# One batch's theta and weight transposes in another order, two casts on another engine, and the last tile cut three to one

## The chip, the cores and the metric

The kernel runs on one core of a Trainium2 chip. The metric is the device time of one execution in microseconds (us). Four timed runs of the kernel before gave 169.96, 170.08, 170.22 and 171.64 us, a median of 170.15. A core has a matrix engine (PE, whose weight loads are listed apart as PEld), a vector engine (DVE), a scalar engine (ACT), GpSimd (POOL) and SyncE (SP), which in this kernel only issues DMAs. Each engine works through its own queue in order.

## What is computed

The inputs are q, k and v (4 batches, 8 heads, 768 tokens, 64 per head) and four weight matrices, all float32. First comes a retention (a linear attention with a decay for each head), whose output for all heads of a token is its row of x, 512 wide:

```
for t in range(S):
    state = gamma * state + outer(k[t], v[t])      # per batch and head, 64 x 64
    y[t]  = scale * q[t] @ state
x = y, heads side by side                          # (4, 768, 512)
```

Then a mixing layer:

```
theta  = x @ w_theta
zr, zi = x * cos(theta), x * sin(theta)
u      = x + w_tok_r @ zr + w_tok_i @ zi           # over the tokens of a batch
out    = u + relu(u @ w_ch)
```

## The kernel before, in words

**Tiling.** A batch's 768 tokens are 6 chunks of 128, or 3 pairs of chunks. There are 12 pairs in all, n = 0 to 11; pair n belongs to batch n // 3. The output is made in 24 tiles of 128 tokens, m = 0 to 23. Matrix work is in bf16 with float32 sums in PSUM. The program writes out the order by hand: each engine runs its instructions in the order in which the calls below stand, and the semaphore waits are put in by the framework.

**A pair.** `load` (L76) brings k, q and v of a pair, 512 KB each, all through SP's queue, into a ring of seven buffers (`pair`). `prep` (L162) makes bf16 copies: k is only cast, by one engine (ACT L169, or POOL or DVE L171); q and v are multiplied by a decay factor in two halves (L175), and the pair of engines given says who takes each half: DP is DVE and POOL, PP is POOL twice. `flip` (L179) transposes k or q on PE and copies the result on DVE; from pair 7 on k, and from pair 10 on q, is transposed by a DMA instead (`flip_dma`, L193). `ret_A` and `ret_mask` make the masked scores, `ret_Y` multiplies them with v, `ret_I` adds the part from the state, `ret_S` and `state_out` update the state. `ret_out` (L278) copies the two halves of the transposed x out of PSUM. `x_pe` (L294) turns x into rows on PE, or `x_dma` (L288) with a DMA for pairs from 5 on. `theta` (L309) is four matmuls and two sines on ACT; `zmul` (L319), on DVE, makes the z of one chunk.

**A tile.** `moe_M(m, lo, hi)` (L327) is the token mix: for each of a batch's six chunks two matmuls 512 columns wide (L340). It needs the transposed token weights of its tile (`w_flip`, L390, and `w_out`, L399: DVE for the real part, ACT for the imaginary one, unless told otherwise) and z of the chunk. `moe_u` (L344, DVE L347) adds x. u is transposed on PE (`moe_U`) or by a DMA (`moe_U_dma`, L350), `moe_O` (L365) multiplies by w_ch, `moe_out` (L372, DVE) finishes, `store` (L378, SP) writes. The PSUM tile of `moe_M` has one buffer for most tiles, so a tile's first matmul waits until `moe_u` of the tile before it has read that buffer. Transposes and `moe_O` share two PSUM buffers, tag `tr`.

**The order.** L469 to L569 are the start: pairs 0, 1, 2 (batch 0), with pieces of tile 0 and 1 between them, and the preparation of pair 3. From L579 a loop over n = 3 to 12 does pair n beside the finishing of pair n-1 and one or two tiles of an earlier batch: one tile each at n = 3 to 6 (tiles 2 to 5, with tiles 0 and 1 finished at n = 3), two each from n = 7 (tiles 6 and 7 at n = 7, tile 8 and 9 at n = 8, and so on). In each round SP's queue gets, in this order: the DMA transpose of the next k (from n = 6), the load of k of pair n+3, `x_dma(n-1)` (from n = 6), the load of q, the load of v, a store. At the end of a round DVE gets `zmul(n-1, 0)` and `zmul(n-1, 1)`, then, in rounds with two tiles, `moe_u` of the second tile. After the loop the last tiles follow, and `moe_last` (L407) does tile 23, cut in two column halves so that the last steps overlap.

**Lines the prediction touches.** In the start: L547 to L557 (second `ret_Y` of pair 2, its `ret_out`, `w_tok(1)`, chunks 2 and 3 of tile 0, `theta(2, 0)`, `flip(3, "k")`, `theta(2, 1)`). In the loop: L598 to L601 (k, q and v of pair n+1 at the head of the round), L657 to L660 (the same at n = 3), L670 and L671 (k of pair n+2 on ACT). In the tail: L407 to L457.

Of the kernel before, what the change touches and what calls it, by code (L numbers as in the profile page):

```python
# [14 lines left out]
FT = mybir.dt.float32  # L15
BF = mybir.dt.bfloat16
# [16 lines left out]
def kernel(  # L33
# [17 lines left out]
    nc = tc.nc  # L51
    B, H, S, D = q.shape
    dm = H * D
    P = 128
    HP = P // 2
    nT = S // P
    nD = dm // P
# [3 lines left out]
    nG = nT // 2  # L61
# [158 lines left out]
    def ret_Y(n, two):  # L220

        if two == 0:
            st[n, "y"] = [psum.tile([P, NP, P], FT, name="yT_ps", tag="acc", bufs=2)
                          for _ in range(2)]
        yT, at, vp = st[n, "y"], st[n, two], st[n, "v"]
        for j in range(NP):
            for a in range(2):
                half = slice(a * HP, (a + 1) * HP)
                for par in range(2):
                    h = 2 * j + par  # L230
                    nc.tensor.matmul(yT[a][par * D:(par + 1) * D, j, :],  # L231
                                     vp[half, two, h * D:(h + 1) * D],
                                     at[half, par, j, :],
                                     start=(two == 0 and j == 0),
                                     stop=(two == 1 and j == NP - 1),
                                     skip_group_check=True)

    def ret_I(n, a):

        c = 2 * (n % nG) + a  # L240
        half = slice(a * HP, (a + 1) * HP)
        yT = st[n, "y"][a]
        if c > 0:
            for j in range(NP):
                nc.tensor.matmul(yT[:, j, :], stbd[c % 2][:, j, :],  # L245
                                 st[n, "qT"][:, :, j, half], start=False,
                                 stop=False, skip_group_check=True)
# [71 lines left out]
    def zmul(n, a):  # L319
        b, g = divmod(n, nG)  # L320
        c = 2 * g + a
        nc.vector.tensor_mul(zs[b][:, c], st[n, "cs", a], _bcast_mid(xs[b][:, c, :], 2))  # L322
# [80 lines left out]
    def w_tok(t0):  # L403
        for r in range(2):
            w_flip(r, t0)

    def moe_last(m):  # L407

        b, t0 = divmod(m, nT)
        hw = dm // 2  # L410
        y_ps = [psum.tile([P, hw], FT, name="y_ps", tag="y", bufs=1),
                psum.tile([P, hw], FT, name="y_ps", tag="acc", bufs=2)]
        u = work.tile([P, dm], BF, name="u", bufs=5)
        uT = work.tile([P, nD, P], BF, name="uT", bufs=4)

        def prods(e):
            for s0 in range(nT):
                for r in range(2):
                    nc.tensor.matmul(y_ps[e], wT[r][:, s0, t0 * P:(t0 + 1) * P],  # L419
                                     zs[b][:, s0, r, e * hw:(e + 1) * hw],  # L420
                                     start=(s0 == 0 and r == 0),
                                     stop=(s0 == nT - 1 and r == 1))
            nc.vector.tensor_add(u[:, e * hw:(e + 1) * hw], y_ps[e],
                                 xs[b][:, t0, e * hw:(e + 1) * hw])

        def flip_u(e):
            u_ps = psum.tile([P, 2, P], BF, name="u_ps", tag="tr", bufs=2)
            for j in range(2):
                jj = 2 * e + j
                nc.tensor.transpose(u_ps[:, j, :], u[:, jj * P:(jj + 1) * P], ident)  # L430
            nc.scalar.copy(uT[:, 2 * e:2 * e + 2, :], u_ps)  # L431

        moe_U_dma(m - 1)
        prods(0)
        moe_O(m - 2)
        moe_out(m - 2)
        store(m - 2)
        prods(1)
        flip_u(0)
        moe_O(m - 1)  # L440
        moe_out(m - 1)
        store(m - 1)
        flip_u(1)
        o_ps = [psum.tile([P, hw], FT, name="o_ps", tag="st", bufs=1),
                psum.tile([P, hw], FT, name="o_ps", tag="acc", bufs=2)]
        for js in ((0, 1), (2, 3)):
            for e in range(2):
                for j in js:
                    nc.tensor.matmul(o_ps[e], uT[:, j, :],
                                     wch[:, j, e * hw:(e + 1) * hw], start=(j == 0),  # L450
                                     stop=(j == nD - 1))
        for e in range(2):
            ot = work.tile([P, hw], FT, name="oh", bufs=2)
            nc.vector.scalar_tensor_tensor(ot, o_ps[e], 0.0, u[:, e * hw:(e + 1) * hw],
                                           ALU.max, ALU.add)
            (nc.sync, nc.scalar)[e].dma_start(
                out=out[b, t0 * P:(t0 + 1) * P, e * hw:(e + 1) * hw], in_=ot)  # L457
# [86 lines left out]
    ret_Y(2, 0)  # L544
    ret_I(2, 0)
    ret_I(2, 1)
    ret_Y(2, 1)  # L547
    ret_out(2, 0, AC.copy)
    ret_out(2, 1, DV.tensor_copy)
    zmul(1, 1)  # L550
    w_tok(1)
    moe_M(0, 2, 3)
    prep(3, "k", (PL,))
    moe_M(0, 3, 4)
    theta(2, 0)
    flip(3, "k")
    prep(3, "q", DP)  # L557
    theta(2, 1)
    x_pe(2)
    w_flip(0, 2, False)  # L560
    w_out(0, 2, AC.copy)
# [17 lines left out]
    for n in range(nG, B * nG + 1):  # L579
        mine, done = tiles_of[n], tiles_of[n - 1]  # L580
        late, two = n > nG, len(mine) > 1
        nxt = n + 1 in pairs

        if nxt and n + 1 >= K_DMA:
            flip_dma(n + 1, "k")
        if n + 3 in pairs:
            load(n + 3, "k")
        if n >= U_DMA:
            moe_U_dma(done[1])
        def preps(engines):  # L590
            prep(n + 1, "q", engines)
            prep(n + 1, "v", PP)
            if n in (nG, nG + 1):
                w_cast(n - nG + 4)

        if n == nG:
            nc.gpsimd.tensor_copy(wch, wdma["ch"])
        if n == nG + 1:  # L598
            prep(n + 1, "k", (PL,))
        if nxt and n > nG:  # L600
            preps(PP)  # L601
        if late:
            ret_I(n - 1, 1)

        if n in pairs:
            ret_A(n, 0)
            ret_mask(n, 0)
        if n == nG:
            moe_M(0, 5, nT)
            w_flip(1, 2)  # L610
            moe_u(0)
            moe_M(1, 4, nT)
            moe_u(1)
        if late:
            ret_Y(n - 1, 1)
            ret_S(n - 1, 1)
            ret_out(n - 1, 0, nc.scalar.copy)
            ret_out(n - 1, 1, nc.scalar.copy)
            state_out(n - 1, 1)
            if n - 1 >= X_DMA:  # L620
                x_dma(n - 1)
        if n + 3 in pairs:
            load(n + 3, "q")

        first = mine[0]
        moe_M(first, 0, 3 if two else 2)
        if late:
            theta(n - 1, 0)
            if n - 1 < X_DMA:
                x_pe(n - 1)  # L630
            theta(n - 1, 1)
        if two:
            moe_M(first, 3, nT)
            moe_u(first)
        for name, limit in (("k", K_DMA), ("q", Q_DMA)):
            if nxt and nG + 1 < n + 1 < limit:
                flip(n + 1, name)
        if n + 1 >= K_DMA and not two:
            moe_M(first, 2, 4)
        if nxt and n + 1 >= Q_DMA:  # L640
            flip_dma(n + 1, "q")
        if n + 3 in pairs:
            load(n + 3, "v")
        for t in tiles_of[n - 2]:
            store(t)
        if n + 1 >= U_DMA:
            moe_U_dma(first)

        if n in pairs:
            ret_S(n, 0)  # L650
            state_out(n, 0)
            ret_A(n, 1)
            ret_mask(n, 1)
            ret_Y(n, 0)
            ret_I(n, 0)
        if n < U_DMA:
            moe_U(done)  # L657
        if n == nG:
            prep(n + 1, "k", (AC,))
            preps(DP)  # L660
        if n == nG or n + 1 < K_DMA and not two:
            moe_M(first, 2, 4)
        if n < nG + 3:
            w_tok(n - nG + 3)
        if not two:
            moe_M(first, 4, nT)
            moe_u(first)
        elif n in pairs:
            moe_M(mine[1], 0, nT)
        if n + 2 in pairs and n > nG:  # L670
            prep(n + 2, "k", (AC,))  # L671
        if late:
            zmul(n - 1, 0)
            zmul(n - 1, 1)
        if two and n in pairs:
            moe_u(mine[1])
        for i, t in enumerate(done):
            if n == nG:
                flip(n + 1, "kq"[i])
            moe_O(t)  # L680
            moe_out(t)
        if n not in pairs:
            moe_M(mine[1], 0, nT)
            moe_u(mine[1])
# [43 lines left out]
```

## Time and profile before

One execution was profiled. Its own time is 170.84 us, of which the trace's span is 169.1; the other 1.74 us lie around the span.

| | |
|---|---|
| median of four timed runs | 170.15 us |
| profiled execution | 170.84 us, span 169.1 |
| PE busy | 155.9 us, 92% of the span |
| DVE, ACT, POOL busy | 101.5, 80.1, 65.7 us |
| read and written in HBM | 25.69 and 6.29 MB |
| k cast on POOL (L171) | 3 times, 1.04 us each |
| k cast on ACT (L169) | 9 times, 1.05 us each |
| half of q on DVE, on POOL (L175) | 5 times 0.91 us, 19 times 1.12 us |
| DMA transpose of x (`x_dma`) | 7, median 3.3 us from issue to landing |

How to read it: "busy" counts the instructions of an engine, not the time in which it waits. A wait in a row of the timeline stands in brackets behind it, with what ended it. The chain of waits goes back from the last instruction of all to what released it, step by step; what isn't in the chain did not set the end. PE is busy nearly throughout, so what counts is where it isn't, and who ended each of those gaps.

### The profile page before, as it was taken

How to read it: one execution, taken by the hardware profiler on the slowest of the kernel's cores; microseconds unless marked ns; L12 is line 12 of the kernel's file. 1: busy time of each engine (PE TensorE's matmuls, PEld its weight loads, DVE VectorE, ACT ScalarE, POOL GpSimd, SP SyncE). 2: the span in 40 equal slices, each digit the busy share in tenths (PEclk: the TensorE clock that was granted, in tenths of full speed). 3: DMA queues.
4: the chain of work that ended last, by engine and by line, in shares of the span. 5: the costliest groups of instructions: out<-in, count | busy, mean ns of one | idle time of the engine just before them, and what ended most of it. 6: DMA issues, size and time to landing. Idle time of an engine off the chain costs nothing.

```text
span 169.1 us, 4659 instructions
## 1 busy us (share of the span) xinstructions
PE 155.9 (92%) x1949; PEld 88.9 (53%) x1975; DVE 101.5 (60%) x137; ACT 80.1 (47%) x138; POOL 65.7 (39%) x83
## 2 busy tenths in 40 slices
PE   7969897698999999999997999999999999999990
PEld 2345665464666667555653654555545544444560
DVE  2358897969584687854926672864727435344451
ACT  8216567371719776696835727547083350000010
POOL 6274859685696787480727144000000000000000
PEclk9999999999999999999999999999999999999997
DMA  4999999989999999999999998959645161753433
GB/s 126 306 342 311 322 330 351 291 305 305 310 305 325 288 264 309 312 197 296 230 293 223 281 277 175 232 65 241 61 94 139 31 186 31 232 113 93 134 116 126
DMA packets 66789, 37.92 MB, mean 224 GB/s; under 512 B 24144, under 2 KB 61264, under 8 KB 66768
## 3 DMA queue, kind: packets, MB, share of 16 engines
q1 hardware_dynamic: 66624, 37.50, 87.3%
q8 instruction: 15, 0.25, 0.6%
q10 hardware_dynamic: 144, 0.13, 0.2%
q14 instruction: 6, 0.05, 0.1%
HBM read 25.69 MB, written 6.29 MB: 189 GB/s over the span
## 4 chain that ended last, share of the span: by engine, by line
PE 77%; DVE 10%; DMA 6%; issue 2%; POOL 1%; DVEq 0%; SPq 0%; POOLq 0%
PE y_ps L340 33%; PE o_ps L368 11%; PE th_ps L312 11%; PE at_ps L208 4%; PE kq_ps L183 3%; DMA pair<-in_q_dram 3%; DVE z L322 3%; PE yT_ps L231 3%; DMA x_sb<-xT 3%; DVE at L215 3%; PE st_ps L262 3%; PE yT_ps L245 3%; PE w_ps L393 2%; DVE kqT L187 2%; PE y_ps L419 2%
## 5 line engine op out<-in xcount | busy, mean ns | idle before, releaser
L340 PE MATMUL y_ps<-z,wtr 128*128 128x512 bf16 x133 | 50.5, 379 | 3.0 <-DVE u L347 1.1
L340 PE MATMUL y_ps<-z,wti 128*128 128x512 bf16 x122 | 46.2, 379 | 0.4 <-issue 0.2
L175 POOL TENSOR_TENSOR kqb<-pair,qscp 128x512 bf16<-128x512 f32 x19 | 21.0, 1121 | 29.3 <-DMA pair<-in_q_dram 22.0
L215 DVE TENSOR_TENSOR at<-at_ps,maskp 128x1024 bf16<-128x1024 f32 x24 | 29.2, 1219 | 4.4 <-PE at_ps L208 4.4
L347 DVE TENSOR_TENSOR u<-y_ps,x_sb 128x512 bf16<-128x512 f32 x23 | 15.9, 690 | 25.0 <-PE y_ps L340 24.9
L175 POOL TENSOR_TENSOR kqb<-pair,vscp 128x512 bf16<-128x512 f32 x24 | 25.5, 1084 | 3.5 <-DMA pair<-in_v_dram 3.5
L285 ACT CAST xT<-yT_ps 128x512 bf16<-128x512 f32 x20 | 13.4, 736 | 28.3 <-PE yT_ps L231 28.3
L312 PE MATMUL th_ps<-wth,xT 128*128 128x512 bf16 x93 | 23.2, 379 | 0.2
L375 DVE SCALAR_TENSOR_TENSOR ot<-o_ps,u 128x512 f32<-128x512 f32 x23 | 15.8, 689 | 12.4 <-PE o_ps L368 12.3
L368 PE MATMUL o_ps<-wch,uT 128*128 128x512 bf16 x92 | 22.8, 379 | 0.2
L340 PEld LDWEIGHTS <-wti 128*128 128x128 bf16 x138 | 13.5, 98 | 15.5 <-issue 2.4
L322 DVE TENSOR_TENSOR z<-cs,x_sb 128x1024 bf16<-128x1024 bf16 x24 | 17.8, 771 | 5.8 <-DMA x_sb<-xT 5.7
L276 ACT CAST stbd<-st_ps 64x256 bf16<-64x256 f32 x40 | 14.7, 367 | 13.3 <-PE st_ps L262 12.4
L315 ACT ACTIVATE cs<-th_ps,halfpi 128x512 bf16<-128x512 f32 x24 | 16.5, 688 | 9.4 <-PE th_ps L312 8.9
L340 PEld LDWEIGHTS <-wtr 128*128 128x128 bf16 x138 | 13.5, 98 | 13.6
L316 ACT ACTIVATE cs<-th_ps,zerob 128x512 bf16<-128x512 f32 x24 | 16.5, 686 | 0.0
L312 PEld LDWEIGHTS <-xT 128*128 128x128 bf16 x96 | 9.0, 98 | 10.6 <-DVE xT L285 0.6
L368 PEld LDWEIGHTS <-uT 128*128 128x128 bf16 x92 | 8.8, 98 | 10.3 <-ACT uT L361 0.4
L187 DVE COPY kqT<-kq_ps 128x1024 bf16<-128x1024 bf16 x16 | 10.8, 686 | 4.8 <-PE kq_ps L183 4.8
L208 PE MATMUL at_ps<-kqT 64*64 64x128 bf16 x384 | 10.6, 221 | 2.6 <-DVE at L215 1.8
L431 ACT COPY uT<-u_ps 128x256 bf16<-128x256 bf16 x2 | 0.7, 372 | 25.5 <-PE u_ps L430 25.5
L183 PEld LDWEIGHTS <-kqb 128*128 128x128 bf16 x136 | 8.7, 99 | 5.3 <-DVE kqb L175 0.8
(61 smaller groups left out, 166.7 us busy)
## 6 DMA issues: line engine op xcount, KB each, us to landing
pair<-in_k_dram SPq DMA_DIRECT2D x12, 512.0 KB, 7.0
pair<-in_q_dram SPq DMA_DIRECT2D x12, 512.0 KB, 7.6
pair<-in_v_dram SPq DMA_DIRECT2D x12, 512.0 KB, 7.8
out_dram<-ot SPq DMA_DIRECT2D x23, 256.0 KB, 2.4
wtok<-in_moe_w_tok_r_dram SPq DMA_DIRECT2D x6, 384.0 KB, 6.6
wtok<-in_moe_w_tok_i_dram SPq DMA_DIRECT2D x6, 384.0 KB, 6.4
w<-in_moe_w_theta_dram SPq DMA_DIRECT2D x1, 1024.0 KB, 8.1
w<-in_moe_w_ch_dram SPq DMA_DIRECT2D x1, 1024.0 KB, 8.6
```

The source lines that it names most:

```text
L175: engines[two].tensor_mul(dst[:, two], src[:, two], _bcast_last(sc[:, 2 * g + two], D))
L208: nc.tensor.matmul(at_ps[half, par, j, :], kT[rows, two, j, half], qT[rows, :, j, half], start=(j == 0), stop=(j == NP - 1), skip_group_ch ...
L215: nc.vector.tensor_mul(at.rearrange("p a j t -> p (a j) t"), at_ps.rearrange("p a j t -> p (a j) t"), _bcast_mid(maskp[:, two].rearrange(" ...
L276: nc.scalar.copy(stbd[(c + 1) % 2][sl, :, sl], st_ps[b][sl])
L312: nc.tensor.matmul(th_ps, st[n, "xT"][:, a, j, :], wth[:, j, :], start=(j == 0), stop=(j == NP - 1))
L315: nc.scalar.activation(cs[:, 0, :], th_ps, AF.Sin, bias=halfpi, scale=1.0)
L316: nc.scalar.activation(cs[:, 1, :], th_ps, AF.Sin, bias=zerob, scale=1.0)
L322: nc.vector.tensor_mul(zs[b][:, c], st[n, "cs", a], _bcast_mid(xs[b][:, c, :], 2))
L340: nc.tensor.matmul(y_ps, wT[r][:, s0, t0 * P:(t0 + 1) * P], zs[b][:, s0, r, :], start=(s0 == 0 and r == 0), stop=(s0 == nT - 1 and r == 1))
L347: nc.vector.tensor_add(u, mo[m]["y"], xs[b][:, t0, :])
L368: nc.tensor.matmul(o_ps, mo[m]["uT"][:, j, :], wch[:, j, :], start=(j == 0), stop=(j == nD - 1))
L375: nc.vector.scalar_tensor_tensor(ot, mo[m]["o"], 0.0, mo[m]["u"], ALU.max, ALU.add)
```

## The change

Three edits.

1. *Start.* The PE transposes of the token weights for tile 1 stand before the second `ret_Y` of pair 2, and their copies out of PSUM behind the two `ret_out`. The matmuls of tile 0 with chunk 3 go behind `theta(2, 1)`. The cast of k of pair 3 stands a few lines earlier, at the same place of POOL's own queue.
2. *Loop, n = 4 and 5.* q and v of pairs 5 and 6 (and k of 5) are no longer prepared at the head of the round but behind `ret_out` and `state_out`; half of q goes to DVE (two instructions that POOL did). The cast of k of pair 6 goes from ACT, at the end of round 4, to POOL, in round 5. On DVE the new half of q stands behind the first mask of the round and ahead of the copy of `x_pe`. On POOL the order is k, half of q, v, weight casts. No DMA is moved on SP's queue; the loads of v of pairs 7 and 8 wait for DVE too, as their buffers held the q that DVE now reads.
3. *Last tile.* Cut in 384 and 128 columns of y and u in place of 256 and 256; u's transposes are three and one, and the last matmuls take three and one. The output's halves stay 256 wide.

```diff
     def moe_last(m):
-        hw = dm // 2
-        y_ps = [psum.tile([P, hw], FT, name="y_ps", tag="y", bufs=1),
-                psum.tile([P, hw], FT, name="y_ps", tag="acc", bufs=2)]
+        cut = (nD - 1) * P
+        cols = (slice(0, cut), slice(cut, dm))
+        y_ps = [psum.tile([P, cut], FT, name="y_ps", tag="y", bufs=1),
+                psum.tile([P, P], FT, name="y_ps", tag="acc", bufs=2)]
...
-                                     zs[b][:, s0, r, e * hw:(e + 1) * hw],
+                                     zs[b][:, s0, r, cols[e]],
...
-            nc.vector.tensor_add(u[:, e * hw:(e + 1) * hw], y_ps[e],
-                                 xs[b][:, t0, e * hw:(e + 1) * hw])
+            nc.vector.tensor_add(u[:, cols[e]], y_ps[e], xs[b][:, t0, cols[e]])
-        def flip_u(e):
-            u_ps = psum.tile([P, 2, P], BF, name="u_ps", tag="tr", bufs=2)
-            for j in range(2):
-                jj = 2 * e + j
-                nc.tensor.transpose(u_ps[:, j, :], u[:, jj * P:(jj + 1) * P], ident)
-            nc.scalar.copy(uT[:, 2 * e:2 * e + 2, :], u_ps)
+        def flip_u(lo, hi):
+            u_ps = psum.tile([P, hi - lo, P], BF, name="u_ps", tag="tr", bufs=2)
+            for j in range(lo, hi):
+                nc.tensor.transpose(u_ps[:, j - lo, :], u[:, j * P:(j + 1) * P], ident)
+            nc.scalar.copy(uT[:, lo:hi, :], u_ps)
...
-        flip_u(0)
+        flip_u(0, nD - 1)
...
-        flip_u(1)
+        flip_u(nD - 1, nD)
...
-        for js in ((0, 1), (2, 3)):
+        for js in (range(nD - 1), (nD - 1,)):
...
     ret_I(2, 1)
+    w_flip(0, 1, False)
+    w_flip(1, 1, False)
     ret_Y(2, 1)
     ret_out(2, 0, AC.copy)
     ret_out(2, 1, DV.tensor_copy)
+    w_out(0, 1)
+    w_out(1, 1)
     zmul(1, 1)
-    w_tok(1)
+    prep(3, "k", (PL,))
     moe_M(0, 2, 3)
-    prep(3, "k", (PL,))
-    moe_M(0, 3, 4)
     theta(2, 0)
     flip(3, "k")
     prep(3, "q", DP)
     theta(2, 1)
+    moe_M(0, 3, 4)
     x_pe(2)
...
-        if n == nG + 1:
-            prep(n + 1, "k", (PL,))
-        if nxt and n > nG:
+        if nxt and n > nG + 2:
             preps(PP)
...
             state_out(n - 1, 1)
+            if n < nG + 3:
+                prep(n + 1, "k", (PL,))
+                preps(DP)
...
-        if n + 2 in pairs and n > nG:
+        if n + 2 in pairs and n > nG + 1:
             prep(n + 2, "k", (AC,))
```

More of the change, by code (lines that the diff above doesn't have):

```diff
@@ L442, in moe_last @@
         store(m - 1)
-        flip_u(1)
+        flip_u(nD - 1, nD)
+        hw = dm // 2
         o_ps = [psum.tile([P, hw], FT, name="o_ps", tag="st", bufs=1),
                 psum.tile([P, hw], FT, name="o_ps", tag="acc", bufs=2)]
-        for js in ((0, 1), (2, 3)):
+        for js in (range(nD - 1), (nD - 1,)):
             for e in range(2):
```

## The prediction, made before the changed kernel was run

> **What bounds the kernel now.** I read the page first, then the chain of waits in order of time, then SP's own timeline, then the timelines of PE, DVE and POOL around the places that are edited.
>
> ```profile
> PE 155.9 (92%) x1949; PEld 88.9 (53%) x1975; DVE 101.5 (60%) x137; ACT 80.1 (47%) x138; POOL 65.7 (39%) x83
> PE   7969897698999999999997999999999999999990
> DMA  4999999989999999999999998959645161753433
> ```
>
> PE is the bound, but the DMA engines are full for the first 60% of the span (each digit is a slice of 4.2 us). The digits can't say which of the two sets the end; the chain does:
>
> ```profile
> 82.35 0.41 PE kq_ps L183 x8
> 82.76 4.97 DMA x_sb<-xT
> 88.08 0.34 issue
> 88.43 0.68 DVE z L322
> 89.11 0.61 DVE u L347
> 89.77 0.38 PE y_ps L340
> ```
>
> From 43 us to the end the chain is PE throughout except here, in round n = 8. PE's first matmul of tile 8 waits 1.10 us (88.67 to 89.77) for `moe_u` of tile 7, which stands on DVE behind two `zmul` of pair 6, and these wait for the DMA transpose of pair 6's x, landed at 87.7. Whether PE could be there earlier doesn't matter, unless that DMA is earlier. SP's timeline (start, duration) says why it is not:
>
> ```profile
> 76.25 0.38 SPq L81 DMA_DIRECT2D pair<-in_q_dram  x1
> 76.69 0.89 SPq L81 DMA_DIRECT2D pair<-in_v_dram  x1
> 77.69 1.36 SPq L380 DMA_DIRECT2D out_dram<-ot  x1
> 79.15 2.88 SPq L195 DMA_TRANSPOSE kqT<-kqb  x1
> 82.12 0.53 SPq L81 DMA_DIRECT2D pair<-in_k_dram  x1
> 82.76 2.02 SPq L290 DMA_TRANSPOSE x_sb<-xT  x1
> ```
>
> SP's rows stand end to end, here and back to 0.8 us. Pair 6's xT was ready when ACT ended its copies (77.71 + 1.32 = 79.03), its transpose was issued 3.7 us later: the queue was late, not the data. So up to 89.77 a lead of PE is worth nothing and a loss of up to 1.10 us costs nothing.
>
> One more landing binds, in round 3: q of pair 4, for which POOL waited 1.46 us and DVE started at the same moment.
>
> ```profile
> 44.43 1.59 POOL L175 TENSOR_TENSOR kqb<-pair,qscp 128x512 bf16<-128x512 f32 x1 [1.46 <-DMA pair<-in_q_dram]
> 44.43 0.68 DVE L175 TENSOR_TENSOR kqb<-pair,qscp 128x512 bf16<-128x512 f32 x1
> ```
>
> **The change, part by part.**
>
> *Start.* PE is idle twice here: 0.55 us before `ret_Y(2, 1)`, and 0.78 before chunk 3 of tile 0:
>
> ```profile
> 30.92 0.42 PE L231 MATMUL yT_ps<-at,kqb 64*64 64x128 bf16 x16 [0.55 <-DVE at L215]
> 33.10 0.38 PE L340 MATMUL y_ps<-z,wtr 128*128 128x512 bf16 x1 [0.78 <-DVE z L322]
> ```
>
> The 12 transposes take 0.67 us (the chain's row at 56.97, "PE w_ps L393 x12") and fill the first gap: 30.37 to 31.04, so `ret_Y` starts 0.12 later and ends at 31.44. The two copies to xT (0.75, on ACT and DVE at once) end at 32.25. Meanwhile PE does chunk 2 (two matmuls of 0.216, z ready at 31.46) to 31.9, and waits to about 32.3 for xT. Then theta 0.86 (33.15), `flip(3, "k")` 0.45 (33.6; POOL's cast ended at 32.51, ACT's copy that frees the PSUM buffer ends at 33.0), theta 0.86 (34.45), chunk 3 0.43 (34.9). Its z is ready in time: DVE does xT to 32.25, the weight copy 0.54, z 0.68 to 1.00, that is 33.8 at the latest. The next step, `x_pe(2)`, stood at 35.70: a lead of 0.8. Behind the DVE work that follows it may grow to 1.2 by the end of tile 1, as chunk 5 of tile 0 (39.88, released by a z of 1.22 us) moves with DVE.
>
> In round 3 the lead meets q of pair 4. DVE can't start its half before 44.43 and ends it at 45.11; behind it in DVE's queue is the copy of tile 3's weights (45.24 before, now 45.11, to 45.67), which frees the PSUM buffer that `flip(4, "k")` needs: 45.75 in place of 46.31. So 0.55 of the lead is left. Both ends: nothing, if DVE's order gives no more than the 0.13; 1.2, if q lands sooner. I take 0.55, the sum of the rows.
>
> *Rounds 4 and 5.* POOL loses two halves of q (1.12 each) and gains one cast of k (1.04); ACT loses a cast (1.05) at 58.37; DVE gains two halves (0.68 to 0.91). SP's order is the same. Pair 5's q landed when POOL started on it (51.70), and POOL's two halves ended at 53.74, just before the transposes of q (54.07). With a lead of 0.55 PE would have waited about 0.3; halves side by side end by 52.8. So this part keeps the lead, and brings nothing of itself: PE has no gap above 0.16 between 50 and 70. What DVE's half is put ahead of: the copy of `x_pe(4)`. First mask to 50.9 with the lead, q 51.7 to 52.4, the copy can start at 52.4, where `x_pe` ends: no delay. In round 5 the copy (62.73 before) can be late by 0.3, as the new cast of k on POOL (58.05 to 59.09) falls beside the two z (59.15 before): z beside a busy POOL took up to 1.68 in place of 1.28 for two (68.92). PE would wait those 0.3 before `flip(6, "q")`. Cost at the end: nothing, since round 8 covers 1.10 + 0.55 = 1.65 us; without that cover, 0.3. The two loads that now wait for DVE's halves were issued at 60.31 and 66.16, 8 and 3 us after the halves end. ACT's free 1.05 is worth nothing: its next copies (60.20) waited for PE.
>
> The Trainium skill ("SBUF — State Buffer", the section on engine ports) says that DVE with two SBUF inputs and GpSimd take a shared port by an exclusive lock, the second waiting out the first. The z of 1.22 and 1.53 us (against 0.68) beside POOL's casts agree. By that rule each z of round 4 could lose the whole 1.04 of the cast; it would still lie under round 8.
>
> *Round 8.* x of pair 6 lands at 87.7, DVE's two z and u follow (89.71), PE starts tile 8 at 89.77 as before. The gap of 1.10 becomes 1.65. The start's and the rounds' parts are worth 0 at the end.
>
> *Last tile.* Here all counts:
>
> ```profile
> 162.94 1.03 PE L368 MATMUL o_ps<-wch,uT 128*128 128x512 bf16 x4
> 163.92 1.24 PE L449 MATMUL o_ps<-wch,uT 128*128 128x256 bf16 x8
> 164.01 0.69 DVE L375 SCALAR_TENSOR_TENSOR ot<-o_ps,u 128x512 f32<-128x512 f32 x1 [0.55 <-PE o_ps L368]
> 164.98 0.76 DVE L454 SCALAR_TENSOR_TENSOR oh<-o_ps,u 128x256 f32<-128x256 f32 x2 [0.28 <-PE o_ps L449]
> ```
>
> Matmuls 256 wide follow at 0.109, 512 wide at 0.216, transposes (128 wide, each with its own weights) at 0.056. So 12 x 384 columns take 1.95 and 12 x 128 take 0.67: 2.62, as 2 x 1.31 before. `moe_O(21)` moves from 160.66 to 161.30, its `moe_out` on DVE from 161.72 to 162.36 and ends at 163.05. `moe_O(22)` takes the PSUM buffer that this frees: 163.10 in place of 162.94, ending its issue at 163.97. One transpose 0.06; ACT's last copy (128x128, 0.27 by the line through 0.372 for 256 and 0.585 for 512) ends at 164.50. Six last matmuls of 0.109 run from 164.02 to 164.67, so the 0.19 that PE waited for ACT (164.36 to 164.55) is gone, and the last two end their issue at 164.89, 0.1 earlier than before. On DVE `moe_out(22)` moves from 164.01 to 164.16, ends at 164.85, and the first output half starts at 165.00 in place of 164.98. Sum: +0.02. Bounds: -0.1, if `moe_O(22)` doesn't wait for DVE; +0.5, if the 12 narrow matmuls go at the pace of a weight load, 98 ns in the rows (12 x 0.042). I take 0.056, the pace of the nearest row, the 12 weight transposes.
>
> The Trainium skill speaks against this cut ("TensorE: Matmul & The Clock Gate", on what sets sustained throughput): weight load and matmul pairs 128 wide go at about 81 ns. Estimate by that page: 12 x 25 ns = +0.3 us. No row here has 128-wide products with changing weights; the transposes have the same shape.
>
> **Sum.** 0 + 0 + 0.02: the profiled execution's 170.84 would become 170.86. It stands 0.69 above the median of 170.15, to which I carry the difference: 170.17, so 170.2.
>
> **Rivals.**
>
> 1. *The lead comes through.* If x of pair 6 lands earlier in an execution without a profile, or follows PE, round 8 has no wait and 0.55 (up to 1.2) is gained: 169.6 (169.0). For: the runs are 0.69 below the profiled one, perhaps out of that 1.10. Against: SP's rows without a gap; 0.4 of wait would still be left, and a wait can't pass a lead on.
> 2. *Slower by the tail.* The narrow products cost 98 ns each, +0.5: 170.7. For: PEld rows of 98 ns. Against: 12 transposes in 0.67. It decides from 60 ns each on.
> 3. *Slower by DVE's half of q.* DVE reaches the half of pair 6 late and SP's load of v (pair 8, at 66.16) waits, with every DMA behind it, pair 6's x among them: one us for each us that the half ends past 66.2, where I have it at 62.9. At +2 us past that: 172. Against: 3 us of room.
> 4. *The edits of the start do nothing*, as q's landing cancels them already in round 3: 170.2 as well, with no lead left at 50 us.
>
> **How the numbers follow.** Forecast with rival 4 0.55, rival 1 0.2, rival 2 0.18, rival 3 0.07. About 1% (1.7 us) is what a measurement of this kernel tells from no change; rival 1 at its largest with -0.1 in the tail hardly reaches it (169.0), rival 2 does not, rival 3 can: faster 0.04, within 0.89, slower 0.07. The range reaches from rival 1's far end with the tail's gain (169.0) to rival 2 with 0.3 for round 5's delay showing (171.0).
>
> **What would show it.** Right: tile 8 starts at 89.8 with a wait near 1.6 us, again behind x of pair 6; `x_pe(2)` near 34.9; `flip(4, "k")` near 45.75; tail within 0.1. Wrong: tile 8 starting before 89.3 (then rival 1), matmuls of the last tile's narrow part over 60 ns apart (rival 2), SP's load of v of pair 8 after 67 us (rival 3).

## The result, and the profile after

The changed kernel took 169.95 us (median), the kernel before 170.47 us in the same comparison. The ratio is 0.9964, with a 95% interval of 0.9947 to 0.9982: about 0.6 us faster (0.3 to 0.9), where no change was forecast. Here and below a ratio leaves out runs over 1.5% above the fastest of their kernel. The profiled execution went from 170.84 to 170.53 us, its span from 169.13 to 168.81.

Where the span went, in stretches that both traces have, in us:

| stretch | before | after |
|---|---|---|
| start to the first matmul of tile 8 | 89.77 | 90.08 |
| from there to the first matmul of the last tile | 69.58 | 69.59 |
| from there to the end of DVE's last output half | 6.38 | 6.40 |
| from there to the end of the span | 3.40 | 2.74 |

The forecast ended its sum with the third row. The gain of 0.66 us is in the fourth.

The page of the changed kernel, the same lines as before:

```profile
PE 156.0 (92%) x1949; PEld 88.2 (52%) x1975; DVE 104.4 (62%) x139; ACT 79.2 (47%) x137; POOL 65.3 (39%) x82
PE   7869897898898998999999999999999999999991
DMA  4999999999999999999999997888636161654344
```

PE, the bound, is as busy as before. ACT has one instruction fewer (138 to 137): the cast of k of pair 6 that went to POOL. This is the line that decides, and it doesn't look like it.

The chain of waits of the changed kernel around tile 8 (start, length, what):

```profile
85.87 2.32 PE y_ps L340 x10
88.19 0.86 PE o_ps L368 x4
89.06 0.22 PE yT_ps L245 x4
89.28 0.35 PE at_ps L208 x16
89.63 0.22 PE yT_ps L231 x16
89.85 0.25 PE st_ps L262 x16
90.10 0.36 PE y_ps L340
```

The DMA transpose of x and the two z are gone from the chain: PE reaches tile 8 at 90.08 by its own timeline, 1.4 later than before (88.67), and waits for nothing. Pair 6's x landed at 88.04 (87.72 before). The forecast had PE at about 88.1 and a wait of 1.65. SP's timeline of the changed kernel, answering to the one of before, again has its rows close behind each other, with gaps of at most 0.53 us:

```profile
76.04 0.99 SPq L81 DMA_DIRECT2D pair<-in_v_dram  x1
77.56 0.39 SPq L380 DMA_DIRECT2D out_dram<-ot  x1
78.20 2.32 SPq L195 DMA_TRANSPOSE kqT<-kqb  x1
80.61 0.52 SPq L81 DMA_DIRECT2D pair<-in_k_dram  x1
81.25 3.73 SPq L290 DMA_TRANSPOSE x_sb<-xT  x1
```

The transpose of pair 6's x was issued 1.51 us earlier than before (81.25 against 82.76), and landed 0.32 later. So the late issue was not what kept x back, or not it alone: from issue to landing it took 4.96 us before and 6.79 after.

Why PE is later is seen in rounds 4 and 5 of the changed kernel, first in the timeline of PE and then in that of DVE (wait and releaser in brackets):

```profile
54.68 0.61 PE L183 MATMUL kq_ps<-ident,kqb 128*128 128x128 bf16 x8 [0.43 <-DVE x_sb L306]
65.32 0.61 PE L183 MATMUL kq_ps<-ident,kqb 128*128 128x128 bf16 x8 [0.77 <-DVE x_sb L306]
```

```profile
52.80 1.22 DVE L175 TENSOR_TENSOR kqb<-pair,qscp 128x512 bf16<-128x512 f32 x1 [1.33 <-DMA pair<-in_q_dram]
53.95 0.68 DVE L306 COPY x_sb<-x_ps 128x1024 bf16<-128x1024 bf16 x1
59.70 2.13 DVE L322 TENSOR_TENSOR z<-cs,x_sb 128x1024 bf16<-128x1024 bf16 x2
63.48 1.18 DVE L175 TENSOR_TENSOR kqb<-pair,qscp 128x512 bf16<-128x512 f32 x1
64.59 0.68 DVE L306 COPY x_sb<-x_ps 128x1024 bf16<-128x1024 bf16 x1
```

DVE's half of q of pair 5 starts at 52.80, half a microsecond after q landed (52.30, and 51.56 before). The two halves take 1.22 and 1.18 where 0.68 to 0.91 was reckoned, and the copy of `x_pe` stands behind it; that copy frees the PSUM buffer which PE's transposes of q need. Before, no wait of PE above 0.2 us lay between 50 and 88 us. In this execution no lead of the start was left to be spent: `flip(4, "k")` stood at 46.34, against 46.31 before, as q of pair 4 landed 0.75 later. The waits put PE behind.

The end, from the timelines of ACT, of the kernel before and then of the changed one. An "ACTq" row is ACT's issue of a DMA, here of the second half of the last output:

```profile
165.76 1.14 ACTq L456 DMA_DIRECT2D out_dram<-oh  x1
```

```profile
166.10 0.37 ACTq L456 DMA_DIRECT2D out_dram<-oh  x1
```

The same 128 KB: 1.14 us of issue before, 0.37 after. It lands at 168.28 before (2.52 after the issue's start) and 167.98 after (1.88), and the span ends 0.8 behind the landing in both. The first half, issued by SP, takes 0.33 in both. What else happens at that moment is in the DMA table for a window; here 165.3 to 165.8 of the kernel before, and then 167.6 to 168.2 of the changed one (packets, MB, share):

```profile
q1 hardware_dynamic: 41, 0.08, 43.8%
q14 instruction: 1, 0.01, 3.8%
```

```profile
q14 instruction: 1, 0.01, 4.0%
q10 hardware_dynamic: 2, 0.00, 0.2%
```

A queue named "instruction" brings one packet of 8 KB. Before, it runs from 165.38 to 165.69, just ahead of the long issue. After, none runs there: it runs from 167.68 on, when ACT's last DMA has long been issued.

### The profile page after: what moved, and what is told of

Its sections match the earlier page's. It is cut to its first block, busy times and chain, and to the rows that moved or that the text cites. A ratio compares the mean times of both kernels' runs of the same rounds, so it can differ in the third digit from the quotient of the medians.

```text
span 168.8 us, 4660 instructions
## 1 busy us (share of the span) xinstructions
PE 156.0 (92%) x1949; PEld 88.2 (52%) x1975; DVE 104.4 (62%) x139; ACT 79.2 (47%) x137; POOL 65.3 (39%) x82
## 4 chain that ended last, share of the span: by engine, by line
PE 65%; DMA 14%; SPq 9%; DVE 4%; issue 3%; POOL 3%; DVEq 0%; POOLq 0%
PE y_ps L340 30%; PE o_ps L368 10%; PE th_ps L312 8%; SPq L81 5%; DMA pair<-in_k_dram 5%; DMA pair<-in_q_dram 5%; DMA w<-in_moe_w_ch_dram 4%; PE at_ps L208 3%; SPq L95 3%; PE yT_ps L245 2%; PE yT_ps L231 2%; PE st_ps L262 2%; PE kq_ps L183 2%; PE y_ps L420 2%; DVE at L215 1%
## 5 line engine op out<-in xcount | busy, mean ns | idle before, releaser
L175 POOL TENSOR_TENSOR kqb<-pair,qscp 128x512 bf16<-128x512 f32 x17 | 19.0, 1131 | 30.4 <-DMA pair<-in_q_dram 19.4
L175 POOL TENSOR_TENSOR kqb<-pair,vscp 128x512 bf16<-128x512 f32 x24 | 25.0, 1062 | 3.9 <-DMA pair<-in_v_dram 3.7
L183 PE MATMUL kq_ps<-ident,kqb 128*128 128x128 bf16 x136 | 10.6, 219 | 2.9 <-DVE x_sb L306 1.2
L430 ACT COPY uT<-u_ps 128x384 bf16<-128x384 bf16 (+1 forms) x2 | 0.7, 372 | 25.5 <-PE u_ps L429 25.5
```

The costliest lines, as they stand in the source:

```text
L175: engines[two].tensor_mul(dst[:, two], src[:, two], _bcast_last(sc[:, 2 * g + two], D))
L183: nc.tensor.transpose(ps[:, two, j, :], st[n, name][:, two, j * P:(j + 1) * P], ident)
```

## The experiments

**Theory 1:** ACT's instructions come in blocks; where ACT reaches a new block just at its last DMA, the issue waits for the fetch and the end is 0.5 to 0.7 us longer. One ACT instruction fewer moves the crossing behind that DMA. Start, rounds and last tile bring nothing themselves. **Rivals:** the gain is the start's lead, the rounds' new order, or the last tile's cut.

All twelve, and the two kernels, by their profiled executions (us): when PE was ready for tile 8, when x of pair 6 had landed, the start of tile 8, the length from the last tile's first matmul to the end of the span, and ACT's last issue; then the ratio of the timed runs to the kernel before.

| kernel | PE ready | x landed | tile 8 | last tile | ACT issue | ratio |
|---|---|---|---|---|---|---|
| before | 88.67 | 87.72 | 89.77 | 9.78 | 1.14 | 1 |
| after | 90.08 | 88.04 | 90.08 | 9.14 | 0.37 | 0.9964 [0.9947, 0.9982] |
| e1 last tile alone | 90.28 | 87.85 | 90.28 | 9.61 | 0.97 | 1.0018 [0.9978, 1.0058] |
| e2 start alone | 87.76 | 86.33 | 88.37 | 9.53 | 0.90 | 0.9931 [0.9891, 0.9972] |
| e3 loop alone | 89.02 | 86.75 | 89.02 | 9.02 | 0.37 | 0.9933 [0.9902, 0.9964] |
| e4 after, ACT +1 | 89.66 | 87.34 | 89.66 | 9.62 | 0.96 | 0.9998 [0.9959, 1.0037] |
| e5 before, ACT +8 | 89.28 | 87.04 | 89.28 | 9.03 | 0.37 | 0.9982 [0.9943, 1.0022] |
| e6 start, ACT +8 | 87.63 | 86.58 | 88.63 | 9.01 | 0.37 | 0.9940 [0.9911, 0.9968] |
| e7 before, u first | 88.62 | 88.15 | 88.62 | 9.53 | 0.88 | 0.9985 [0.9956, 1.0013] |
| e8 after, u first | 90.03 | 87.66 | 90.03 | 9.14 | 0.37 | 0.9970 [0.9938, 1.0002] |
| e9 start, ACT +8, u first | 88.22 | 87.53 | 88.22 | 9.02 | 0.37 | 0.9869 [0.9814, 0.9923] |
| e10 after, q on POOL | 89.69 | 87.72 | 89.76 | 9.17 | 0.37 | 0.9971 [0.9937, 1.0005] |
| e11 before, one cast moved | 88.88 | 87.98 | 90.02 | 9.02 | 0.38 | 0.9941 [0.9905, 0.9976] |
| e12 before, both halves by SP | 88.66 | 88.17 | 90.21 | 9.59 | (SP: 0.54) | 0.9971 [0.9941, 1.0000] |

Two things hold for all: from tile 8 to the last tile it is 69.58 to 69.60 us in every one, and the landing of x of pair 6 moves by up to 1.84 us (86.33 to 88.17) from execution to execution, also between kernels whose order up to there is the same (87.04 to 88.17 in before, e1, e5 and e12). So single spans can't be compared; the stretches can.

**e1: the last tile's cut alone.**

```diff
-        hw = dm // 2
+        cut = (nD - 1) * P
+        cols = (slice(0, cut), slice(cut, dm))
...
-        for js in ((0, 1), (2, 3)):
+        for js in (range(nD - 1), (nD - 1,)):
```

> The kernel before with the last tile's new cut alone. Theory 1 (the gain is ACT's instruction fetch: in the profile of before, ACT's issue of the very last DMA takes 1.14 us while 8 KB of instructions are fetched at 165.38, in the changed kernel 0.37 and the fetch comes later, as ACT has one instruction fewer): ACT has as many instructions as before, so its last issue stays above 1 us and the ratio is 1.000 within 0.001. Theory 2 (PE's lead of the start passes round 8 in executions without a profile): 1.000 too. Theory 3 (the cut itself is worth it): 0.996. DVE's last instruction ends within 0.1 us of where it stood, counted from the tile's first matmul, by all of them but theory 3.

Measured: ratio 1.0018 [0.9978, 1.0058]; from the last tile's first matmul to DVE's last half 6.39 us, against 6.38. The cut brings nothing up to there, and ACT's issue stays long (0.97).

**e2: the start's order alone.**

```diff
+    w_flip(0, 1, False)
+    w_flip(1, 1, False)
     ret_Y(2, 1)
...
+    w_out(0, 1)
+    w_out(1, 1)
     zmul(1, 1)
-    w_tok(1)
+    prep(3, "k", (PL,))
     moe_M(0, 2, 3)
-    prep(3, "k", (PL,))
-    moe_M(0, 3, 4)
...
     theta(2, 1)
+    moe_M(0, 3, 4)
```

> The kernel before with the new order of the start alone. Theory 1: ACT's instruction count is unchanged, ratio 1.000 within 0.001, ACT's last issue above 1 us. Theory 2: 0.55 us of lead come through, ratio 0.997. Theory 3: 1.000. In the profile by theory 1: x_pe(2) near 35.0 and flip of k of pair 4 0.3 to 0.6 us earlier relative to the landing of q, and tile 8 still starting two us after x of pair 6 has landed.

Measured: `x_pe(2)` at 34.82 (before 35.70), PE ready for tile 8 at 87.76, and held there 0.61 us by u behind x's transpose, in the profiled execution as forecast. Its row in PE's timeline:

```profile
88.37 0.38 PE L340 MATMUL y_ps<-z,wtr 128*128 128x512 bf16 x1 [0.61 <-DVE u L347]
```

But the timed ratio, 0.9931 [0.9891, 0.9972], is below 1 although ACT's issue is long here (0.90). That ratio rests on seven of the twelve timed runs; the median of all twelve is 170.25, against 170.30 for the kernel before in the same comparison. So a gain of the start by itself is not shown.

**e3: the loop's edits alone.**

```diff
-        if n == nG + 1:
-            prep(n + 1, "k", (PL,))
-        if nxt and n > nG:
+        if nxt and n > nG + 2:
...
+            if n < nG + 3:
+                prep(n + 1, "k", (PL,))
+                preps(DP)
...
-        if n + 2 in pairs and n > nG:
+        if n + 2 in pairs and n > nG + 1:
```

> The kernel before with the change of rounds 4 and 5 alone (k of pair 6 cast on GpSimd, half of q on DVE). Theory 1: ACT has one instruction fewer, its last issue takes about 0.4 us and the ratio is 0.996. Theory 2 and theory 3: 1.000, as this part has no lead of its own and leaves the tail as it was.

Measured: ratio 0.9933 [0.9902, 0.9964], ACT's issue 0.37, last tile 9.02. PE has no wait above 0.2 us in rounds 4 and 5. Not the missing lead explains this, as `flip(4, "k")` stood at 46.44, nearly as in the changed kernel (46.34); but q of pair 5 landed at 50.64, 1.66 us earlier. The part of the change that was costed at nothing is the one that shortens the end.

**e4: the changed kernel with one ACT instruction more**, a copy of one column ahead of the last tile.

```diff
+    nc.scalar.copy(sin0, zerob)
     moe_last(last_m)
```

> The changed kernel with one more ACT instruction, a copy of one element a partition to a spare tile, ahead of the last tile, where ACT has been idle for over 15 us. Theory 1: ACT's last issue is back above 1 us and the whole gain is lost, ratio 1.000 to the kernel before. Theories 2 and 3: the gain stays, 0.996.

Measured: ratio 0.9998 [0.9959, 1.0037]; ACT's issue back at 0.96, the packet of the instruction queue back ahead of it (165.13), last tile 9.62. By the profile one copy of 0.2 us, which ACT does 28 us before its last DMA (138.0 and 165.7), takes the short end away. The ratio agrees, though its interval overlaps the changed kernel's.

**e5: the kernel before with eight such copies.**

```diff
+    nc.scalar.copy(sin0, zerob)
+    nc.scalar.copy(sin0, zerob)
...
     moe_last(last_m)
```

> The kernel before with eight more ACT instructions (copies of one element a partition to a spare tile) ahead of the last tile, where ACT has been idle for over 15 us, and nothing else. Theory 1 (ACT's instruction fetch): with eight more instructions in its queue ACT crosses the same block of instructions earlier, in that idle time, the fetch is done before the last DMA, whose issue takes about 0.4 us in place of 0.9 to 1.1; from the last tile's first matmul to the end 9.1 us in place of 9.5 to 9.8; ratio 0.9965. More work, less time. Theory 2 (the lead of the start) and theory 3 (the cut of the last tile): 1.000 or above.

Measured: issue 0.37, last tile 9.03; the packet now runs at 136.87, ahead of the copies (137.6 to 139.4). ACT is not idle there, though the expectation says so: it is at its last sines (135.3 to 137.8), and the copies follow them without a gap. The ratio, 0.9982 [0.9943, 1.0022], holds both the expected gain and none. More work on ACT, and the end in the profile is shorter by 0.75: the number of instructions matters and not their time.

**e6: the start with the eight copies** (the diffs of e2 and e5).

> The new order of the start, with the same eight ACT copies. Theory 1, with the body held by x of pair 6: 0.9965, the same as the eight copies alone. Theory 2: the lead of the start comes on top, 0.55 us more, 0.993. The profile tells them apart as well: tile 8's first matmul within 0.2 us of where DVE's u of tile 7 ends (the DMA holds it), or well behind it (PE holds it).

Measured: ratio 0.9940 [0.9911, 0.9968], issue 0.37, last tile 9.01; PE ready at 87.63 and held 1.00 us, to 88.63, by u of tile 7. The lead stands in front of round 8, as forecast. The interval holds both what theory 1 (0.9965) and what theory 2 (0.993) expected, so the timed runs don't tell whether any of the lead comes through.

**e7 and e8: u of tile 7 ahead of the two z of pair 6**, in the kernel before and in the changed one. This takes away what makes tile 8 wait for x of pair 6.

```diff
+        ahead = n == nG + 4
+        if ahead:
+            moe_u(mine[1])
...
-        if two and n in pairs:
+        if two and n in pairs and not ahead:
```

> The kernel before with one pair of DVE steps exchanged: in round 7 u of tile 7 stands ahead of the two z of pair 6, so that tile 8's first matmul no longer waits for the DMA of pair 6's x. If that wait holds the kernel in most executions, as the prediction has it, the ratio is 0.9935 (1.10 us); if PE arrives there late by itself in about half of them, as the profiles of the first four experiments look, 0.997; if the next wait takes it over, 1.000. ACT's last issue stays at 0.9 to 1.1 us.

> The changed kernel with the same exchange in round 7. Where the wait was what kept the start's lead from showing (the prediction's round 8), the lead of 0.55 us now shows on top of ACT's 0.6: 0.993 or less, more below the kernel before with the exchange than the 0.0035 of ACT alone. Where there is no lead left by round 8, 0.9965 less what the exchange itself brings.

Measured: in e7 x landed at 88.15 and u was done at 87.51; tile 8 started when PE was ready (88.62). Still the ratio is 0.9985 [0.9956, 1.0013]. In e8 0.9970 [0.9938, 1.0002], and the time of tile 8 is the changed kernel's, as PE was the last there anyway. The wait of 1.10 us can be taken away, and its removal alone is worth at most 0.75 us (from 0.9956), a smaller gain than was expected (0.9935) if that wait held the kernel in most executions.

**e9: e6 and e7 together.** (The eight copies stand ahead of the last tile, as in e5, not behind the start's work as the expectation has it.)

> The kernel before with the start's order of the change, eight small ACT copies behind the start's work (so that ACT's instruction fetch no longer stands ahead of its last DMA), and u of tile 7 ahead of the two z of pair 6. Output complete. Theory 1 (the end gains by ACT's fetch, the lead is held only by u's place behind the two z): ACT's last DMA issue 0.37 us, tail 9.0 us; tile 8 starts when PE is ready, about 87.7 in an execution that lands x of pair 6 at 86.5 or later, and from there 69.6 us to the last tile; ratio 0.990 to 0.992. Rival (the DMA's pace sets a later place of round 8 as well, so the lead is given back there): the stretch from tile 8 to the last tile grows by up to 0.8 us, ratio 0.9965.

Measured: ratio 0.9869 [0.9814, 0.9923], 168.32 us median of six runs, the fastest of all, also against the changed kernel (0.9964 [0.9947, 0.9982]; the intervals are apart). It is below the 0.990 to 0.992 expected, which the interval holds. The stretch from tile 8 to the last tile is 69.60, so the rival, by which it would grow, fell. e6 and e7 alone would make 0.9925 together. That both edits are worth more than that would fit tile 8's start at the later of PE and u, since only with both do both come earlier (88.22 and 87.11, against 88.67 and 89.71 before); but e6's and e9's intervals overlap, so it is not shown. In the timeline of PE there is no wait in brackets:

```profile
88.22 0.39 PE L340 MATMUL y_ps<-z,wtr 128*128 128x512 bf16 x1
```

**e10: the changed kernel with both halves of q on POOL.**

```diff
-                preps(DP)
+                preps(PP)
```

> The changed kernel with both halves of q of pairs 5 and 6 on POOL in place of half on DVE. Output complete. If DVE's half is what eats the lead in rounds 4 and 5: PE's waits for the x_sb copy (0.43 and 0.77 us in the changed kernel) go, and PE is ready for tile 8 about 1.2 us earlier, near 88.8 for q of pair 4 landing at 45.0; x of pair 6 then holds tile 8, so that the time hardly moves: 0.994 to 0.9965, ACT's last issue still 0.37. Rival (POOL's four halves are late for the transposes of q): the waits come back at the q transposes with POOL as the releaser, PE ready as late as in the changed kernel, ratio 0.9965 to 1.000.

Measured: the wait of 0.43 is gone, the one of 0.77 is 0.49; PE ready at 89.69, 0.9 later than expected and just when u was done (89.71). From `flip(4, "k")` to there it is 43.07 us; it is 43.42 to 44.42 in the three kernels with the whole order of the change up to there (after, e4, e8), and 42.27 to 42.62 in the other ten.

In the four executions with the loop's new order, the loss grows with the time from `flip(4, "k")` to the landing of q of pair 5. In e3 that is 4.20 us, and the stretch is 42.58; in e4 5.69 and 43.42; in the changed kernel 5.96 and 43.74; in e8 6.90 and 44.42. Without the new order the stretch stays within 42.27 to 42.62 while the landing comes 4.42 to 5.84 after. e10, at 5.90, is best set beside the changed kernel: without DVE's half it loses 0.7 us less of some 1.3, by one execution each. DVE's timeline of e10 shows where more of it goes:

```profile
59.57 2.96 DVE L322 TENSOR_TENSOR z<-cs,x_sb 128x1024 bf16<-128x1024 bf16 x2
64.19 0.67 DVE L306 COPY x_sb<-x_ps 128x1024 bf16<-128x1024 bf16 x1
```

The two z, 1.28 us in the kernel before, take 2.96 beside POOL's cast and halves, and the copy is late again. Without the new order they took up to 2.68 (e1), so this is not the new order's alone. The ratio, 0.9971 [0.9937, 1.0005], is the changed kernel's.

**e11: the kernel before with one instruction moved**, the cast of k of pair 6 from ACT to POOL, and nothing else.

```diff
-        if n == nG + 1:
+        if n in (nG + 1, nG + 2):
...
-        if n + 2 in pairs and n > nG:
+        if n + 2 in pairs and n > nG + 1:
```

> The kernel before with one instruction moved: the cast of k of pair 6 from ACT, at the end of round 4, to POOL at the head of round 5. Nothing of the start, of the q halves or of the last tile. Output complete. Theory 1 (ACT's instruction fetch): one ACT instruction fewer puts the fetch behind ACT's last DMA: issue 0.37 us in place of 1.14, tail 9.0 in place of 9.6 to 9.8, ratio 0.9965 (0.995 to 0.998). Rival (the gain is the start's lead or the last tile's cut): issue 0.9 to 1.1, ratio 1.000, or above it if POOL's two halves of q in round 5 come 1.04 us later.

Measured: ratio 0.9941 [0.9905, 0.9976]. ACT's timeline at the end, and PE's at tile 8:

```profile
166.02 0.38 ACTq L456 DMA_DIRECT2D out_dram<-oh  x1
```

```profile
90.02 0.38 PE L340 MATMUL y_ps<-z,wtr 128*128 128x512 bf16 x1 [1.14 <-DVE u L347]
```

Round 8 is as in the kernel before (1.14 against 1.10 of wait), and the last tile is 9.02 against 9.78. The instruction queue's packet runs at 167.46. This one move gives what the change gives, within the intervals.

**e12: both halves of the last output issued by SP.**

```diff
-            (nc.sync, nc.scalar)[e].dma_start(
+            nc.sync.dma_start(
```

> The kernel before with both halves of the last output issued from SP's queue; ACT issues no last DMA. Output complete. Theory 1: the end no longer depends on when ACT fetches instructions: the second half is issued from SP at about 0.35 to 0.4 us a DMA, lands about 1.9 us after the issue, and the tail is 9.0 to 9.3 us in place of 9.6 to 9.8: ratio 0.9965 to 0.998. Rival (the slow end is the landing itself, whichever engine issues it): tail 9.6 us or longer, as the second half also stands behind the first in one queue: ratio 1.000 to 1.003.

Measured: last tile 9.59, where theory 1 had 9.0 to 9.3; ratio 0.9971 [0.9941, 1.0000], undecided. ACT, with nothing left to issue, ended at 164.98, and a packet of the instruction queue ran from 165.98 to 166.70, amid the two halves; it took 0.72 us (0.31 in the kernel before), and the halves landed 2.34 and 2.25 us after their issue (1.78 for SP's half in the kernel before). DMA table of e12, 165.9 to 166.8:

```profile
q1 hardware_dynamic: 150, 0.27, 79.2%
q14 instruction: 1, 0.01, 5.0%
```

Whether that packet slows the halves or both are slow because SP issues them back to back was not tried. The reading "take the DMA off ACT and the end is short" is wrong in this trace.

## Why the prediction was wrong, point by point

**The step that failed** is "ACT's free 1.05 is worth nothing", and with it the sum, which stopped at DVE's last output half and carried the rest of the execution over unchanged. The time of that cast is worth nothing, as said. But it was also one instruction of ACT's row, and by the count alone a packet of instructions moves from just ahead of ACT's last DMA to behind it. The term that the sum had as 0 is -0.66 in the profiles (3.40 to 2.74). Over all thirteen in which ACT issues it, the last issue is 0.88 to 1.14 us in the five with ACT's count as before or put back (before, e1, e2, e4, e7) and 0.37 or 0.38 in the eight with another count; the last tile is 9.61 us on the mean of the former and 9.07 of the latter. e11 and e4 show it from both sides: one instruction less brings the short end, and a gain clear of noise in the timed runs; one more takes the short end away, and leaves a ratio whose interval holds 1. That the packet is ACT's own isn't written in the trace, which names only the queue; it follows from its moving with ACT's count (165.38, 167.46 with one fewer, 136.87 with eight more). That the issue waits for it shows in the five long ones: the issue starts 0.38 to 0.62 us after the packet starts, but always ends 1.50 to 1.52 us after it, so the earlier the packet comes, the shorter is the issue.

The row was there to be seen: 1.14 us of issue for a DMA whose twin on SP took 0.33. It was off the list because the chain of waits ends at DVE, and I read the chain as the end.

The Trainium skill ("Runtime: NRT & Kernel Launch", Instruction fetch mechanics) says that an engine's instruction memory is refilled in blocks of 16 KiB while the current one executes, and that crossing one is mostly hidden. Here the queue in question moved 8 KB at a time, and such a packet at the last DMA was not hidden: 0.5 to 0.8 us of issue.

**The bound and round 8: right for that execution, not for all.** Tile 8 starts at the later of PE and u of tile 7, and u ends 2.0 us after x of pair 6 lands, wherever u stands behind the two z (e2, e6, e11, e12 waited 0.61 to 1.55). But of the five kernels with before's order up to there, PE was the last in two (e1, e5), u in three. In such executions a lead can count, so rival 1 may have had more for it than its 0.2; e6 below e5 (0.9940 against 0.9982) speaks for it, but the intervals overlap. And "the queue was late, not the data" fell: with the issue 1.51 earlier the landing was no earlier.

**The start: right.** `x_pe(2)` at 35.01 and 34.5 to 35.0 in the other kernels with it (forecast 34.9). `flip(4, "k")` came at 46.34, not 45.75, as q of pair 4 landed 0.75 later (45.04, against 44.29). It comes 1.21 behind DVE's start on that q (45.13), where the forecast had 1.32 (45.75 from 44.43).

**Rounds 4 and 5: wrong, though in the profiled execution it cost next to nothing at the end.** "This part keeps the lead" fell: DVE's half starts at 52.80, where 51.70 was reckoned (0.74 of this is q's later landing), and holds DVE for 1.15 us (to 53.95), not 0.7, and the copy of `x_pe` stands behind it. PE lost 1.4 us between `flip(4, "k")` and tile 8 (43.74 against 42.36), where 0.3 was the bound; round 8's wait covered it, as reckoned (u was done at 90.03, PE ready at 90.08). Where q of pair 5 landed early, as in e3, nothing was lost. The Trainium skill's shared port ("SBUF — State Buffer", engine ports) was cited for the z alone; the rows 1.22 (the half), 2.13 and 2.96 (two z) agree with it, and it would have spoken against the half's 0.68 as well. But the 2.13 is no mark of the change: six kernels without the loop's new order took 2.13 for these z too (e5, e6, e7, e9, e11, e12).

**Last tile: right to the hundredth up to DVE, short by 0.1 behind it.** +0.02 forecast, +0.01 to +0.02 measured. The narrow matmuls follow at 0.056, as their rows in PE's timeline of the changed kernel show:

```profile
162.48 0.22 PE L420 MATMUL y_ps<-z,wtr 128*128 128x128 bf16 x1
162.54 0.22 PE L420 MATMUL y_ps<-z,wti 128*128 128x128 bf16 x1
162.59 0.22 PE L420 MATMUL y_ps<-z,wtr 128*128 128x128 bf16 x1
162.65 0.22 PE L420 MATMUL y_ps<-z,wti 128*128 128x128 bf16 x1
```

So rival 2 fell; the skill's 81 ns for such pairs is not what these rows show. But with ACT's issue short, the last tile is 9.14 to 9.17 with the cut and 9.01 to 9.03 without: ACT's half lands 1.88 to 1.89 instead of 1.76 to 1.77 us after its issue. So the cut costs 0.1 us, not by its matmuls. The store of tile 22 stands nearer to the last halves with the cut (0.55 us ahead of the first in the changed kernel, 0.70 in e11), which may be why; this was not tried.

**Rival 3** fell: PE was late, no load was. **Rival 4** fell in e2 and e6: `flip(4, "k")` stood at 45.34 and 45.23, 0.97 and 1.08 earlier than before, of which 0.37 and 0.53 are q's own earlier landing, and PE was ready for tile 8 0.9 and 1.0 earlier. The changed kernel's profiled execution had no such lead.

## What to carry to other kernels

A sum doesn't end at the last compute instruction: the issue and the landing of the last DMA are part of it, and an issue row far longer than its twin on another queue is worth asking after. When an instruction changes its engine, ask what the count does as well as what the time does; a copy of a column on an idle engine, or one instruction fewer, is a cheap test. A start that waits for two things may gain little when only one of them comes earlier, so the edits that bring them have to be timed together. And landings shift from execution to execution: the new order of rounds 4 and 5 cost PE nearly nothing with an early landing (e3), and 2 us with a late one (e8).

## What the runs showed of the hardware that was not expected

- An 8 KB packet of an instruction queue just ahead of ACT's last DMA made the issue 0.88 to 1.14 us long, where it is 0.37 or 0.38 otherwise.
- With no DMA left for ACT, such a packet fell amid the last output and took 0.72 us (e12).
- The same loads land at different times in different executions: q of pair 4 at 43.4 to 45.3 us, x of pair 6 at 86.3 to 88.2, whatever the kernel; so which of PE and DMA is last at tile 8 varies too.
- Two z on DVE in round 5 took 1.28 to 2.96 us, by whether DVE or POOL started first. In the kernel before the second z started at 59.75, 0.10 ahead of POOL's half of q: the z took 0.68, the half 1.48. In e7 the half started 0.12 ahead of the z: the half took 1.10, the z 1.53.
